# Sixteen of the 128 rows of wo's first load taken over by GpSimd, and sixteen small loads set among the large ones: a decode step with windowed attention

## The chip, the cores and the metric

The program runs on one core of one Trainium2 chip. A core has five engines with instruction streams of their own: TensorE (PE; its weight loads are PEld), VectorE (DVE), ScalarE (ACT), GpSimd (POOL) and SyncE (SP), and 16 DMA engines that move data between HBM and the on-chip memory SBUF, which has 128 partitions. The metric is the device time of one execution in microseconds, lower is better; a time is the median of several executions.

## What is computed

One token is decoded for two sequences (B = 2, D = 512). The token is normalised, goes through attention over the last 4096 positions of a cache and an output projection, and is gated by a small MLP:

```python
xn = _layernorm(x, axis=-1)
q = (x @ wq)                       # x here is xn; 32 heads of 128
k = k_cache[:, :, Sk - W:, :]      # Sk = 32768, W = 4096, 8 kv heads, repeated 4 times
v = v_cache[:, :, Sk - W:, :]
p = _softmax(einsum("bhqd,bhkd->bhqk", q, k) * Dh ** -0.5)
s = einsum("bhqk,bhkd->bhqd", p, v) -> (B, 1, 4096) @ wo
g = _silu(_B_ref(xn, w_in, w_sp, b_sp, w_out))
return x + s * g
```

All is float32. Read from HBM are the windows of k and v (32 MB each), wq and wo (8 MB each), w_in (3.5 MB) and w_out (1.75 MB).

## The kernel before, in words

**Loads.** Every large tensor passes through `ring`, a pool of four slots of 32 KB per partition (line 76, `slot` at line 81). In order: win, wout, two halves of wq, then the key and value windows, then wo. A *unit* is one sequence and two of its eight kv heads, so there are eight units (NU = 8). `load_unit` (line 114) loads the keys or the values of one unit, 128 rows of 32 KB, 4 MB in one transfer. The loop at line 416 issues k0, k1, v0, k2, v1, ... k7, v6, v7. Since four slots hold everything, each load from the fifth on waits until the slot's last content has been used: by VectorE's transposes for keys (`turn`, line 305), by TensorE for values (`values`, line 366).

After that comes wo (4096 x 512), split so that partition p holds the rows 32p to 32p + 31, in 32 blocks. It takes three slots, in pieces of 8 and 8 blocks, of 8, and of 4, 2, 1 and 1 (lines 424 to 434). A piece of 8 blocks is 128 partitions by 16 KB. After the second piece x is loaded once more in another layout (`x4`).

**Queues.** All these loads are issued by SyncE, in the order of the code. The names `pe`, `dve`, `act` and `sp` wrap an engine in `InOrder` (line 27), which pins each instruction behind the one before it on its engine; the profile therefore shows most instructions under line 37, the helper's call. `nc.gpsimd` is used without that wrap. ScalarE issues three tiny loads at the start. GpSimd builds masks at the start (lines 125 to 142: `make_identity`, then the memsets of xnT, ones, hT and others) and has nothing to do afterwards.

**Compute.** For each unit the keys are transposed by VectorE, multiplied by TensorE, and the softmax is made one unit behind (lines after 438). The last values give oT. Then 28 blocks of wo go into the bank `part` and the last four into `so` (lines 480 to 497), two small VectorE operations apply the gate and add x, and SyncE stores the result (line 501).

Of the kernel before, what the change touches and what calls it, by code (L numbers as in the profile page):

```python
# [9 lines left out]
F32 = mybir.dt.float32  # L10
# [4 lines left out]
P = 128  # L15
# [27 lines left out]
def kernel(  # L43
# [13 lines left out]
    nc = tc.nc  # L57
    pe, dve, act, sp = (InOrder(tc, e) for e in (nc.tensor, nc.vector, nc.scalar, nc.sync))
    B, _, D = x.shape
    _, HKV, SK, _ = k_cache.shape  # L60
# [8 lines left out]
    NU = B * HKV // 2  # L69
# [7 lines left out]
    cst = ctx.enter_context(tc.tile_pool(name="cst", bufs=1))  # L77
# [3 lines left out]
    def slot(name):  # L81
        return ring.tile([P, SLOT], F32, tag="slot", name=name)
# [18 lines left out]
    for a in range(2):  # L101
        t = slot(f"wq{a}")
# [7 lines left out]
    def by_group(t):  # L110

        return bass.AP(tensor=t.tensor, offset=t.offset, ap=[[DC, G], [D, B], [1, DC]])

    def load_unit(cache, u, name):

        b, w = divmod(u, NU // B)
        t = slot(f"{name}{u}")
        first = cache[b, 2 * w, SK - W :, :]
        src = bass.AP(tensor=first.tensor, offset=first.offset, ap=[[SLOT, P // 2], [SK * DH, 2], [1, SLOT]])
        sp.dma_start(t, src)  # L120
        return t.rearrange("p (j d) -> p j d", d=DH)
# [288 lines left out]
    for n in range(NU):  # L410
# [2 lines left out]
        u.b, u.w = divmod(n, NU // B)  # L413
        units.append(u)

    for n in range(NU + 1):
        if n < NU:
            units[n].k = load_unit(k_cache, n, "k")
        if n > 0:
            units[n - 1].v = load_unit(v_cache, n - 1, "v")  # L420

    wo_v = wo.rearrange("(p j) d -> p j d", j=32)
    blocks = []
    pieces = ((8, 8), (8,), (4, 2, 1, 1))
    j = 0
    for i, piece in enumerate(pieces):
        t = slot(f"wo{i}").rearrange("p (j d) -> p j d", d=D)
        at = 0
        for n in piece:
            sp.dma_start(t[:, at : at + n, :], wo_v[:, j : j + n, :])  # L430
            blocks += [(t, at + a) for a in range(n)]
            at, j = at + n, j + n
            if j == 16:
                sp.dma_start(x4[0:P:16, :], by_group(x))

    prev = old = None
    last = units[-1]
# [44 lines left out]
    for n in range(EARLY):  # L482
        t, a = blocks[n]
# [5 lines left out]
    for n in range(EARLY, 32):  # L489
        if n == LATE:  # L490
            spread_quarters(so, parts, start=False, stop=False)
        t, a = blocks[n]
# [37 lines left out]
```

## Time and profile before

| what | value |
|---|---|
| time, median of 3 runs | 217.89 us (217.43 to 218.01) |
| time of the profiled execution | 217.89 us |
| its span, first to last instruction | 216.1 us |
| PE, DVE, ACT, POOL busy | 153.6, 108.6, 44.0, 2.6 us |
| read from HBM | 89.40 MB, 414 GB/s over the span |
| loads of k: issue to landing | 26.0 us (8 loads of 4 MB) |
| loads of v: issue to landing | 30.6 us (8 loads of 4 MB) |
| SP's DMA instructions | 29 |

The span is what the trace covers; some 1.8 us of the measured time lie around it. In the profile, times in windows and timelines count from the start of the span. "SPq" is SyncE's instruction queue, where a load is issued; q1 is the queue of the DMA engines that these loads fill, q10 the one of ScalarE's loads, q8 and q14 carry the program's own code. "DMA share" is the mean busy share of the 16 DMA engines in a window; in short windows it can stand a little above 1. A line such as `k<-in_A_k_cache_dram` names the tile written and the tensor read.

### The profile page before, as it was taken

To read this page: it belongs to the slowest core of one execution; us is meant where nothing else is said; L and a number is where in the kernel's file an instruction comes from. 1 tells how busy PE (TensorE), PEld (TensorE's weight loads), DVE (VectorE), ACT (ScalarE), POOL (GpSimd) and SP (SyncE) were. 2 spreads that over 40 slices of the span, in tenths; PEclk is the share of its full clock that TensorE was granted. 3 is DMA by queue.
4 is the path that set the end of the run, shared out by engine and by line. 5 is a ranking of instruction groups with operands and counts; after the bars stand their busy time and mean duration, and the time that the engine had idled before them with its cause. 6 is when DMAs were issued, how large, how long until landed. Compare 5 with 4: busy or idle time off the path is not lost.

```text
span 216.1 us, 2228 instructions
## 1 busy us (share of the span) xinstructions
PE 153.6 (71%) x866; PEld 43.1 (20%) x866; DVE 108.6 (50%) x176; ACT 44.0 (20%) x109; POOL 2.6 (1%) x14
## 2 busy tenths in 40 slices
PE   0173185518959957994995699459959967997963
PEld 0121121101212212221221222222222212231311
DVE  2505402569788079338806941685479089331001
ACT  5003310002231331043131304120331241242001
POOL 4000000000000000000000000000000000000000
PEclk9998579955997995899799589856996996999698
DMA  6999999999999999999999999999999999999990
GB/s 256 425 437 467 406 438 422 431 443 419 455 400 473 397 455 412 431 437 419 450 403 461 412 461 403 443 419 425 449 412 452 412 455 412 443 397 425 424 368 26
DMA packets 3929, 89.54 MB, mean 414 GB/s; under 512 B 446, under 2 KB 462, under 8 KB 848
## 3 DMA queue, kind: packets, MB, share of 16 engines
q1 hardware_dynamic: 3912, 89.40, 96.7%
q8 instruction: 7, 0.11, 0.2%
q10 hardware_dynamic: 8, 0.00, 0.0%
q14 instruction: 2, 0.02, 0.0%
HBM read 89.40 MB, written 0.00 MB: 414 GB/s over the span
## 4 chain that ended last, share of the span: by engine, by line
DMA 52%; PE 28%; DVE 18%; issue 1%; DVEq 0%; SPq 0%
DMA k<-in_A_k_cache_dram 38%; DVE kt L37 15%; PE sh L37 9%; PE s L37 8%; DMA wo<-in_A_wo_dram 8%; PE acc L37 6%; DMA win<-in_B_w_in_dram 5%; PE z L37 2%; PE mo L37 1%; PE so L37 1%; DVE m L37 1%; DVE pT L37 1%; PE oT L37 0%; DVE mx L37 0%; PE col L37 0%
## 5 line engine op out<-in xcount | busy, mean ns | idle before, releaser
L37 DVE STREAM_TRANSPOSE kt<-k 128x2048 f32<-128x2048 f32 x32 | 72.7, 2295 | 41.7 <-DMA k<-in_A_k_cache_dram 35.7
L37 PE MATMUL sh<-kt,qbd 128*32 128x512 f32 x256 | 41.4, 710 | 18.4 <-DVE kt L37 18.4
L37 ACT ACTIVATE shs<-sh 128x512 f32<-128x512 f32 x32 | 19.1, 597 | 119.3 <-PE sh L37 119.3
L37 PE MATMUL s<-shs,add_dq 128*128 128x512 f32 x64 | 40.0, 732 | 0.0
L37 PE MATMUL acc<-v,pT 128*32 128x512 f32 x256 | 31.9, 640 | 0.2 <-DVE pT L37 0.2
L37 PEld LDWEIGHTS s<-shs,add_dq 128*128 128x128 f32 x64 | 11.0, 215 | 30.1 <-issue 25.7
L37 PEld LDWEIGHTS sh<-kt,qbd 128*32 128x32 f32 x256 | 6.5, 115 | 38.8 <-issue 24.5
L37 PEld LDWEIGHTS acc<-v,pT 128*32 128x32 f32 x256 | 7.7, 119 | 25.5 <-issue 18.3
L37 PE MATMUL mo<-l,same_r 128*128 128x2 f32 x16 | 3.7, 299 | 10.6 <-ACT p L37 10.6
L37 ACT ACTIVATE o<-acc,wd 128x128 f32<-128x128 f32 x32 | 9.1, 372 | 3.4 <-PE acc L37 3.4
L37 PE MATMUL part<-wo,oT 128*32 128x512 f32 x56 | 8.0, 708 | 2.0 <-DMA wo<-in_A_wo_dram 1.7
L37 ACT ACTIVATE p<-s,nb 128x256 f32<-128x256 f32 x16 | 7.6, 490 | 7.2 <-DVE nb L37 6.9
L37 PE MATMUL q_ps<-wq,xnT 128*32 128x512 f32 x64 | 7.3, 594 | 2.3 <-DMA wq<-in_A_wq_dram 2.3
L37 PE MATMUL col<-o,sel 128*32 128x512 f32 x16 | 8.3, 601 | 0.4 <-ACT o L37 0.4
L37 PE MATMUL z<-win,xnT 128*32 128x448 f32 x32 | 5.3, 836 | 4.5 <-DMA win<-in_B_w_in_dram 4.5
L37 DVE TENSOR_REDUCE m<-s 128x2 f32<-128x512 f32 x8 | 5.4, 670 | 4.9 <-PE s L37 4.9
L37 DVE TENSOR_TENSOR res<-so,gate 128x128 f32<-128x128 f32 x1 | 0.3, 291 | 11.7 <-PE so L37 11.7
L37 PE MATMUL y<-wout,hT 128*32 128x512 f32 x14 | 3.3, 993 | 3.8 <-issue 3.8
L37 DVE STREAM_TRANSPOSE pT<-p 128x512 f32<-128x512 f32 x8 | 5.4, 674 | 1.2 <-ACT p L37 1.2
L37 ACT ACT_TABLE_LOAD x4 | 5.1, 1283 | 1.9 <-issue 1.9
L37 PE MATMUL xnT_ps<-ident,xn 2*128 2x2 f32 x4 | 0.6, 252 | 6.9 <-DVE xn L37 6.9
L37 PEld LDWEIGHTS mo<-l,same_r 128*128 128x128 f32 x16 | 3.0, 233 | 12.2 <-ACT p L37 12.2
(106 smaller groups left out, 63.2 us busy)
## 6 DMA issues: line engine op xcount, KB each, us to landing
k<-in_A_k_cache_dram SPq DMA_DIRECT2D x8, 4096.0 KB, 26.0
v<-in_A_v_cache_dram SPq DMA_DIRECT2D x8, 4096.0 KB, 30.6
wq<-in_A_wq_dram SPq DMA_DIRECT2D x2, 4096.0 KB, 29.7
wo<-in_A_wo_dram SPq DMA_DIRECT2D x3, 2048.0 KB
win<-in_B_w_in_dram SPq DMA_DIRECT2D x1, 3584.0 KB
wout<-in_B_w_out_dram SPq DMA_DIRECT2D x1, 1792.0 KB, 15.0
wo<-in_A_wo_dram SPq DMA_DIRECT2D x1, 1024.0 KB
wo<-in_A_wo_dram SPq DMA_DIRECT2D x1, 512.0 KB, 18.0
```

The lines of the kernel that those rows point to most:

```text
L37: return self.tc.keep_in_program_order(call(*args, **kwargs))
```

## The change

Three things are added or altered.

- *Small loads from SyncE.* `load_rows(n)` loads n rows of 128 bytes of x (n from 1 to 16) into a tile `rows` that nothing reads. One follows most of the large loads of the loop over units (n = 2 to 14 and 1), and two follow wo's third piece (15 and 16). They stand in SyncE's pinned order.
- *The first piece of wo in two parts.* SyncE loads partitions 0 to 111 of it. The partitions 112 to 127 are loaded by GpSimd (`load_rest`) in six transfers of 4, 2, 3, 2, 2 and 3 rows of 16 KB.
- *Fillers.* Before, between and after these stand seven GpSimd transfers of 2, 1, 5, 3, 1, 5 and 15 rows of 4 bytes of x, into a tile `few` that nothing reads. GpSimd's transfers are not pinned in program order.

The bytes of wo, k and v are the same, and so is all arithmetic.

```diff
@@ -413,25 +413,61 @@
         u.b, u.w = divmod(n, NU // B)
         units.append(u)
 
+    rows = cst.tile([16, 16, 32], F32, tag="rows", name="rows")
+
+    def load_rows(n):
+        sp.dma_start(rows[:n, n - 1, :], bass.AP(tensor=x.tensor, offset=x.offset, ap=[[32, n], [1, 32]]))
+
     for n in range(NU + 1):
         if n < NU:
             units[n].k = load_unit(k_cache, n, "k")
+            if n > 0:
+                load_rows(2 * n)
         if n > 0:
             units[n - 1].v = load_unit(v_cache, n - 1, "v")
+            if n < NU - 1:
+                load_rows(2 * n + 1)
+            elif n == NU - 1:
+                load_rows(1)
+
 
     wo_v = wo.rearrange("(p j) d -> p j d", j=32)
     blocks = []
     pieces = ((8, 8), (8,), (4, 2, 1, 1))
+    HEAD = 112
+    few = cst.tile([16, 16], F32, tag="few", name="few")
+    steps = ((0, 2), (4, 0), (0, 1), (2, 0), (0, 5), (3, 0), (0, 3), (2, 0), (0, 1), (2, 0), (0, 5), (3, 0), (0, 15))
+    assert sum(n for n, _ in steps) == P - HEAD
+
+    def load_rest(dst, src):
+        p = HEAD
+        for i, (n, skip) in enumerate(steps):
+            if n > 0:
+                nc.gpsimd.dma_start(dst[p : p + n], src[p : p + n])
+                p += n
+            else:
+                nc.gpsimd.dma_start(
+                    few[:skip, i : i + 1], bass.AP(tensor=x.tensor, offset=x.offset, ap=[[32, skip], [1, 1]])
+                )
+
     j = 0
     for i, piece in enumerate(pieces):
         t = slot(f"wo{i}").rearrange("p (j d) -> p j d", d=D)
         at = 0
         for n in piece:
-            sp.dma_start(t[:, at : at + n, :], wo_v[:, j : j + n, :])
+            dst, src = t[:, at : at + n, :], wo_v[:, j : j + n, :]
+            if j == 0:
+                sp.dma_start(dst[:HEAD], src[:HEAD])
+                load_rest(dst, src)
+            else:
+                sp.dma_start(dst, src)
             blocks += [(t, at + a) for a in range(n)]
             at, j = at + n, j + n
             if j == 16:
                 sp.dma_start(x4[0:P:16, :], by_group(x))
+            if j == 24:
+                load_rows(15)
+                load_rows(16)
 
     prev = old = None
     last = units[-1]
```

## The prediction

> **What bounds the kernel now.** I read the page first: the 40 slices, the DMA queues and the chain that ended last.
>
> ```profile
> span 216.1 us, 2228 instructions
> ...
> DMA  6999999999999999999999999999999999999990
> ...
> q1 hardware_dynamic: 3912, 89.40, 96.7%
> q8 instruction: 7, 0.11, 0.2%
> ...
> DMA 52%; PE 28%; DVE 18%; issue 1%; DVEq 0%; SPq 0%
> ```
>
> The DMA engines are full from the second slice to the last but one. The queue that SyncE feeds (q1) moves 89.40 MB in 96.7% of 16 engines' span: 89.40 MB / (0.967 x 16 x 216.1 us) = 26.7 GB/s for one engine, so a row of 16 KB (one partition of half of wo's first slot) takes 16384 / 26.7 = 0.61 us of its engine. The chain of waits gives only 52% to DMA, but its waits alternate with work that runs under the stream, so the stages by window say more:
>
> ```profile
> core 0: us, PE busy (x) PEld busy (x) DVE busy (x) ACT busy (x) POOL busy (x), PEclk, DMA share, GB/s
> ...
> 2.00:212.00 210.00, 152.79 (x854) 42.82 (x858) 107.42 (x172) 43.87 (x109) 1.18 (x4) 0.85 0.99 425
> ```
>
> From 2 to 212 us the engines are busy 99%. No faster arithmetic shortens this; what sets the end is when the last of the 16 engines has moved its share. The chain's last pieces show the tail behind it:
>
> ```profile
> 193.00 18.05 DMA wo<-in_A_wo_dram
> 211.05 0.04 issue
> 211.09 1.25 PE so L37 x32
> 212.34 0.01 issue
> 212.35 0.47 PE so L37 x8
> ```
>
> The output projection follows the last loads of wo. How evenly the engines finish is seen in quarter-microsecond windows (column before the last: busy share of 16 engines):
>
> ```profile
> 209.50:209.75 0.25, 0.00 (x0) 0.00 (x0) 0.00 (x0) 0.00 (x0) 0.00 (x0) 1.00 1.07 410
> 209.75:210.00 0.25, 0.14 (x4) 0.15 (x8) 0.00 (x0) 0.00 (x0) 0.00 (x0) 1.00 0.74 279
> 210.00:210.25 0.25, 0.25 (x4) 0.01 (x2) 0.00 (x0) 0.00 (x0) 0.00 (x0) 1.00 0.52 197
> 210.25:210.50 0.25, 0.25 (x8) 0.00 (x0) 0.00 (x0) 0.00 (x0) 0.00 (x0) 1.00 0.55 213
> 210.50:210.75 0.25, 0.25 (x4) 0.00 (x0) 0.00 (x0) 0.00 (x0) 0.00 (x0) 1.00 0.47 180
> 210.75:211.00 0.25, 0.17 (x4) 0.00 (x0) 0.00 (x0) 0.00 (x0) 0.00 (x0) 1.00 0.41 156
> 211.00:211.25 0.25, 0.16 (x8) 0.16 (x12) 0.00 (x0) 0.20 (x1) 0.00 (x0) 1.00 0.38 147
> 211.25:211.50 0.25, 0.25 (x16) 0.21 (x8) 0.00 (x0) 0.25 (x1) 0.00 (x0) 1.00 0.28 107
> 211.50:211.75 0.25, 0.25 (x15) 0.05 (x8) 0.00 (x0) 0.14 (x1) 0.00 (x0) 1.00 0.07 25
> 211.75:212.00 0.25, 0.25 (x12) 0.25 (x16) 0.00 (x0) 0.00 (x0) 0.00 (x0) 1.00 0.02 8
> ```
>
> It is a staircase. Half of the engines (0.52) have nothing left at about 210.0, six (0.38 x 16) still work at 211.2, the last stops near 211.9: the early half waits almost 2 us for the late ones, though all got the same bytes. The seven packets on q8 load code: 0.2% of 16 x 216.1 us is 6.9 us, 1.0 us each, and whichever engine carries one falls behind by about that. That fits six or seven late engines.
>
> **The change part by part.** The profiled run took the median's own 217.89 us: 216.1 us of span and 1.79 us around it. The sum is made against that.
>
> (a) *A row fewer on the late engines.* SyncE loads 112 of 128 rows, seven an engine where it was eight; GpSimd brings the other 16 in six transfers of 4, 2, 3, 2, 2 and 3, with seven fillers of 2 to 15 tiny rows between, as if to steer each onto chosen engines. If the steering holds, the late engines keep one row less: -0.61 us, and the early ones, with one more, end at 210.0 + 0.61, still ahead. The staircase area from 209.75 on is 0.86 us of all 16 engines, so a perfect levelling would end at 210.6, 1.3 us sooner; one row cannot reach that. I take -0.61; from 0 (nothing shifted) to -0.61.
>
> (b) *Small loads.* Sixteen more SyncE loads of 1 to 16 rows of 128 bytes: 136 rows, 8.5 per engine on average, at most 16 on one. Their price comes from the output store, eight rows of 512 bytes and the counter writes of its four engines, 12 packets:
>
> ```profile
> 214.50:215.50 1.00, 0.00 (x0) 0.00 (x0) 0.00 (x0) 0.00 (x0) 0.00 (x0) 0.50 0.02 4
> ```
>
> 0.02 x 16 us / 12 is 0.027 us a packet. A row and its counter write are 0.05 us; 8.5 of them +0.45 us on the engine that ends last, from +0.05 (one) to +0.86 (sixteen). What the issues cost SyncE is in its timeline, the list of DMA issues and its waits:
>
> ```profile
> 170.15 0.66 SPq L37 DMA_DIRECT2D x<-in_A_x_dram  x1
> ...
> k<-in_A_k_cache_dram SPq DMA_DIRECT2D x8, 4096.0 KB, 26.0
> ...
> SPq L37 <- DMA k<-in_A_k_cache_dram: 26.2, 8, 5.3
> ```
>
> On SyncE each issue takes up to 0.66 us (the small load of x), and a big load behind it starts that much later. It is hidden by the queue: a 4 MB load needs 4194304 / 16 / 26.7 = 9.8 us of the engines and lands 26.0 us after its issue, so some 16 us of other loads lie ahead. Without that cover all sixteen issues would cost 10.6 us. SyncE already waits for earlier loads (26.2 us in 8 waits) before it overwrites one of four slots; should the small loads make a counter come round sooner, the load then waited for is about the one whose slot is refilled anyway, so I add nothing for it. Only the last 2048-byte pieces of wo could be held until the first pieces have landed, and those lie 4 MB ahead of them in the stream.
>
> (c) *Thirteen GpSimd transfers.* No transfer of that engine is in this trace. If each also leaves a counter write on every engine, 13 x 0.027 = +0.35 us; if only where it moves rows, about 0.1. I take +0.2. The timelines of SyncE, TensorE and GpSimd:
>
> ```profile
> 169.29 0.81 SPq L37 DMA_DIRECT2D wo<-in_A_wo_dram  x2
> ...
> 201.23 5.04 PE L37 MATMUL part<-wo,oT 128*32 128x512 f32 x32 [0.35 <-issue]
> ...
> 2.23 0.95 POOL L142 MEMSET oT<- 128x1024 f32 x1
> ...
> 0.87 0.20 POOL L127 MEMSET xnT<- 128x128 f32 x1
> 1.10 0.29 POOL masks.py:199 TENSOR_SCALAR_AFFINE_SELECT ident<-ident 128x128 f32<-128x128 f32 x1
> ```
>
> GpSimd is idle from 3.2 us on (2.23 + 0.95). Its real transfers wait for the same release of the slot as SyncE's, at 169.29; nothing stands behind them there, and TensorE first uses wo at 201.2, so their issue time costs nothing.
>
> (d) *Where the 16 rows land.* They go to 16 neighbouring partitions while the stream is at 99%. Until now each engine wrote rows that only it wrote at that time, all engines at full pace. Now several engines fill the same few partitions that others are filling. The trace has no such case. Bounds: nothing, if only the engine's own pace counts; and 16 x 0.61 = 9.8 us if the rows follow one another through one path and hold its regular engine back all the while. The nearest row is one transfer of this change: its largest has four neighbouring rows, and if these share one path with that path's own stream, it is put back by 4 x 0.61 = +2.45 us. I take this, as between no sharing and all on one the four are what the change itself issues together, and no cover exists: the stream has no gap in which an engine could catch up, and a late engine ends the kernel.
>
> [...]
>
> Sum: -0.61 + 0.45 + 0.2 + 2.45 = +2.5 us, **220.4 us**. Its own range: with the small terms at their bounds and (d) between 1.2 (half of the four rows meet traffic) and twice 2.45, 218.6 to 223.4.
>
> **The rivals.**
> 1. *It works: not slower.* The moved rows run freely; the late six end 0.61 us sooner. For it: every transfer in the trace runs at one pace, and the list fits the staircase: fillers and rows dealt in turn round 16 engines give seven engines two rows, two one and seven none. It decides as long as fewer than 0.61 / 0.027 = 22 small packets fall on the engine that ends; at the middle values 0.65 us they cancel it. 217.3 to 217.9; I say 217.6.
> 2. *The change doesn't do what it says.* The code makes the identity mask before it clears xnT, but the last two rows above show L127 ahead of masks.py:199: on that engine the order of the program is not kept. Fillers wait for nothing, real rows for a slot until 169 us; if the fillers all go first, nothing is steered, the late engines keep what they had, and without (d) (b) and (c) remain: +0.65, 218.5 (217.9 to 219.1).
> 3. *Each GpSimd transfer stalls the engines as a code load does.* A q8 packet takes 1.0 us against 0.61 for 16 KB: 0.38 more. Thirteen on every engine: 4.9 us, with (b) and without gain +5.4, 223.3. Against it: the small loads of ScalarE at the start leave no hole in the slices.
> 4. *The 112 rows collide as well.* Seven rows an engine no longer fall on the partitions that an engine had to itself. If each waits for one other row, 7 x 0.61 = 4.3 us more than the forecast: 224.7. [...]
>
> **How the numbers follow.** Forecast 0.38, rival 1 0.20, rival 2 0.15, rival 3 0.12, rival 4 0.15. A measurement of this kernel tells about 0.3% (0.65 us) from no change. Faster by more needs rival 1 with almost no small packets, or more levelling than a row: 0.09. Within 0.3%: the rest of rival 1 and most of rival 2, 0.25. Slower: 0.66. The range goes from 217.3 (rival 1's best) to 225.0 (rival 4); outside lie some 0.1 on either side. It is wide because two cases of no loss hold a third of the chance.
>
> **What would show it.** Right: a dip in DMA share or GB/s between 170 and 197 us, when the 16 rows and the 112 come, a staircase that begins later and is longer than 2 us, and last loads of wo at about 214.4. Rival 1: the same start of the staircase, steeper, over by 211.4. Rival 2: fillers on the timeline near 3 us, and the staircase as it was. Rival 3: low DMA share wherever a GpSimd transfer is issued, fillers too. Rival 4: wo's first pieces land 4 us late, with engines short of full share until then. The forecast is wrong if the share stays 0.99 from 170 to 200 us and the end moves by less than 1 us; (b) is wrong if shares drop around the small loads all along.

## The result and the profile after

The changed kernel takes 234.82 us (median of 4 executions, 234.29 to 236.5) beside 217.95 us for the kernel before (4 executions, 217.43 to 218.16). The ratio is 1.0791, 95% interval 1.0731 to 1.0851: 16.9 us slower. The profiled execution took 234.29 us.

The page of the changed kernel: its span, the 40 slices and the DMA queues (packets, MB, share of 16 engines' span).

```profile
span 232.4 us, 2267 instructions
...
DMA  7999999999999999999999999999999999999910
GB/s 252 419 457 445 434 407 426 440 445 440 400 440 437 445 412 423 440 446 427 401 440 440 443 417 418 440 446 434 403 420 330 367 355 285 228 279 383 363 74 8
...
q1 hardware_dynamic: 4168, 89.16, 94.2%
q0 software_dynamic: 416, 0.26, 0.5%
```

Up to slice 30 (about 174 us) nothing differs from before, though 14 of the sixteen small loads lie there. Then GB/s falls to 228 while the row above still shows 9: the engines are as busy as before and move half as much. Busy share alone would have shown no loss. The new queue q0 is GpSimd's: thirteen transfers left 416 packets, 32 each, whether they carried 1 row or 15.

The same in three stretches. Windows of the kernel before, then of the changed kernel (the last two columns are DMA share and GB/s):

```profile
168.00:188.00 20.00, 16.94 (x80) 4.29 (x72) 11.25 (x13) 5.64 (x14) 0.00 (x0) 0.91 1.02 437
188.00:208.00 20.00, 17.21 (x122) 5.27 (x124) 3.47 (x11) 3.33 (x12) 0.00 (x0) 0.91 0.97 412
208.00:216.00 8.00, 4.01 (x60) 1.20 (x52) 0.58 (x2) 0.60 (x1) 0.00 (x0) 0.90 0.34 130
```

```profile
168.00:188.00 20.00, 16.61 (x79) 4.30 (x72) 11.25 (x13) 5.64 (x14) 3.07 (x6) 0.91 1.02 371
188.00:208.00 20.00, 7.31 (x50) 2.12 (x52) 2.57 (x9) 2.19 (x8) 0.00 (x0) 0.72 0.98 270
208.00:216.00 8.00, 6.71 (x36) 2.15 (x28) 0.75 (x2) 1.14 (x4) 0.00 (x0) 0.84 0.98 391
216.00:224.00 8.00, 6.14 (x40) 1.75 (x44) 0.14 (x1) 0.00 (x0) 0.00 (x0) 0.79 0.64 254
224.00:232.00 8.00, 3.85 (x60) 1.20 (x52) 0.58 (x2) 0.60 (x1) 0.00 (x0) 0.94 0.05 18
```

At the stream's 425 GB/s the missing bytes are worth (437 - 371) x 20 / 425 = 3.1 us in the first stretch and (412 - 270) x 20 / 425 = 6.7 us in the second. The span grew by 16.3 us, so another 6.5 us are tail: from 216 to 224 us only 0.64 of the engines have anything left.

The timeline of the changed kernel, GpSimd and SyncE's issues:

```profile
3.14 3.74 POOL L449 DMA_DIRECT2D few<-in_A_x_dram  x7
...
169.18 0.80 SPq L37 DMA_DIRECT2D wo<-in_A_wo_dram  x2
169.44 3.07 POOL L446 DMA_DIRECT2D wo<-in_A_wo_dram  x6 [162.56 <-PE acc L37]
...
192.76 25.84 SPq L37 DMA_DIRECT2D wo<-in_A_wo_dram  x4
```

All seven fillers left at 3 us, 166 us ahead of the rows between which the code has them. The end of the chain of waits:

```profile
167.17 38.40 DMA v<-in_A_v_cache_dram
205.57 0.02 issue
205.59 21.26 DMA wo<-in_A_wo_dram
226.85 0.04 issue
226.89 1.24 PE so L37 x32
```

The last values take 38.40 us from issue to landing where a load of v took 30.6 before, and the load of wo that ends this chain lands at 226.85 instead of 211.05. SyncE waits too (us in total, times, longest):

```profile
SPq L37 <- DMA v<-in_A_v_cache_dram: 14.4, 2, 12.5
...
SPq L37 <- DMA wo<-in_A_wo_dram: 12.0, 2, 7.6
```

So its last three loads of wo are issued at 205.59, 213.51 and 218.27, where the last one went out at 193.95 before. This is not what costs the time: the engines were still 0.94 busy from 216 to 220 us, and the run below without small loads and fillers, in which only one load was issued that late (at 206.51), takes as long.

### The profile page after: what moved, and what is told of

It is laid out like the page before. It is cut to its first block, busy times and chain, and to the rows that moved or that the text cites. A ratio compares the mean times of both kernels' runs of the same rounds, so it can differ in the third digit from the quotient of the medians.

```text
span 232.4 us, 2267 instructions
## 1 busy us (share of the span) xinstructions
PE 159.0 (68%) x866; PEld 44.3 (19%) x866; DVE 108.5 (47%) x176; ACT 44.0 (19%) x109; POOL 9.4 (4%) x27
## 4 chain that ended last, share of the span: by engine, by line
DMA 57%; PE 24%; DVE 14%; issue 3%; ACT 1%; DVEq 0%
DMA k<-in_A_k_cache_dram 27%; DMA v<-in_A_v_cache_dram 17%; DVE kt L37 11%; DMA wo<-in_A_wo_dram 9%; PE sh L37 5%; DMA win<-in_B_w_in_dram 5%; PE s L37 4%; PE q_ps L37 4%; PE acc L37 4%; PE z L37 2%; PE y L37 2%; PE so L37 1%; PE mo L37 1%; DVE u L37 1%; DVE pT L37 1%
## 5 line engine op out<-in xcount | busy, mean ns | idle before, releaser
L37 PE MATMUL acc<-v,pT 128*32 128x512 f32 x256 | 34.5, 684 | 12.7 <-DMA v<-in_A_v_cache_dram 12.7
L37 PEld LDWEIGHTS acc<-v,pT 128*32 128x32 f32 x256 | 8.3, 125 | 40.3 <-issue 32.3
L37 DVE TENSOR_REDUCE heads<-col 32x128 f32<-32x512 f32 x2 | 1.3, 662 | 20.4 <-PE col L37 20.4
L446 POOL DMA_DIRECT2D wo<-in_A_wo_dram x6 | 3.1, 520 | 162.6 <-PE acc L37 162.6
L37 PE MATMUL q_ps<-wq,xnT 128*32 128x512 f32 x64 | 9.4, 751 | 0.0
```

The lines of the kernel that those rows point to most:

```text
L37: return self.tc.keep_in_program_order(call(*args, **kwargs))
L446: nc.gpsimd.dma_start(dst[p : p + n], src[p : p + n])
```

## The experiments

Fourteen kernels. Where one execution was made it says so; the kernel before beside them took 217.73 us (13 executions, 217.47 to 218.38) for the first eight, 217.97 (9) for the next four and 217.81 (3) for the last two.

**Each part of the change alone.** First the sixteen small loads without the rest: wo's first piece is one load again.

```diff
-                sp.dma_start(dst[:HEAD], src[:HEAD])
-                load_rest(dst, src)
+                sp.dma_start(dst, src)
```

> The sixteen small loads alone; the first piece of wo is one transfer of 128 rows again. Three theories stand. T1, shared ways: engines that write into the same few partitions share their way in, so the loss of 16.9 us comes from where the 112 rows and the 16 rows land. T2: each GpSimd transfer stalls the engines whatever it carries. T3: the small loads cost it. T1 and T2 expect +0.3 to +0.9 us here (8.5 rows per engine at 0.05 us), T3 most of 16.9 us.

217.81 us (10 executions), ratio 0.9999, interval 0.9988 to 1.001. The small loads cost nothing that can be measured.

Then the first piece in two parts, without GpSimd, small loads or fillers: 112 and 16 rows, or 64 and 64, both issued by SyncE.

```diff
-            sp.dma_start(t[:, at : at + n, :], wo_v[:, j : j + n, :])
+            dst, src = t[:, at : at + n, :], wo_v[:, j : j + n, :]
+            for rows in ((0, 112), (112, P)) if j == 0 else ((0, P),):    # or ((0, 64), (64, P))
+                sp.dma_start(dst[slice(*rows)], src[slice(*rows)])
```

> No small loads, no GpSimd: SyncE loads the first piece of wo as 112 rows and then 16 rows. T1 expects +5 to +10 us: seven rows an engine at up to twice 0.61 us (+4.3), and 16 rows that meet in four ways (+2.5) on engines that have fallen out of step. T2 and T3 expect +0.5 us or less.

> No small loads, no GpSimd: SyncE loads the first piece of wo as two halves of 64 rows, four rows an engine in each. T1 expects each half to reach only half of the ways into SBUF, so that the piece takes up to 9.8 us instead of 4.9: about +5 us, with 16 KB packets of about 1.2 us. If only an engine's own pace counts, 0 to +0.2 us and packets of 0.61 us.

224.86 us and 224.41 us (one execution each): +7.1 and +6.7 us for a second transfer of the same bytes. Windows of the two halves:

```profile
188.00:192.00 4.00, 4.00 (x33) 1.18 (x36) 1.40 (x5) 0.34 (x1) 0.00 (x0) 1.00 1.02 291
192.00:196.00 4.00, 2.90 (x30) 1.05 (x26) 1.18 (x4) 1.85 (x8) 0.00 (x0) 1.00 0.98 209
196.00:200.00 4.00, 3.60 (x24) 0.83 (x16) 0.00 (x0) 1.14 (x4) 0.00 (x0) 1.00 0.96 205
200.00:204.00 4.00, 1.44 (x9) 0.96 (x8) 0.89 (x2) 0.00 (x0) 0.00 (x0) 1.00 0.98 242
204.00:208.00 4.00, 3.06 (x16) 0.61 (x16) 0.00 (x0) 0.00 (x0) 0.00 (x0) 0.63 0.99 419
```

Busy 0.96 to 0.98, moving 205 to 242 GB/s: about half the pace for 12 us, from 192 to 204, where the kernel before moved 426 GB/s, and full pace (419) again right after. That a half of the rows reaches only half of the ways into SBUF, and that 16 rows meet in four, was T1's supposition: the windows show the pace, and no run shows a way or how many there are. The loss is larger than the +5 us expected, since more than the piece is slowed: it has 128 packets of 16 KB, and 163 took over 0.8 us.

Next the change without small loads and fillers, so that the split and GpSimd's six transfers remain (both calls of `load_rows` and the filler branch of `load_rest` do nothing).

> The change without its small loads and without the seven fillers: 112 rows from SyncE, 16 rows by six GpSimd transfers. T1 expects nearly all of the loss, +14 to +17 us. T2, by transfers (6 of 13), about half, +7 to +8 us. T3 expects under +2 us.

234.64 us (one execution), +16.9: the whole loss. So neither fillers nor small loads have a part in it. The split explains 7.1; what GpSimd adds was still open.

**What GpSimd's transfers cost beside a whole piece.** The kernel before, with eight more GpSimd transfers of four rows of 8 KB into a spare tile while the last values stream in; once four neighbouring partitions each, once four apart by four.

```diff
...
+    def extra_rows(u):
+        gp.tensor_copy(tick, u.wd[:, 0:1])
+        for rows in [slice(p, p + 4) for p in (80, 84, 88, 92, 112, 116, 120, 124)]:   # or slice(p, p + 13, 4), p = 0, 16, ..
+            gp.dma_start(spare[rows], wo_v[rows, 0:4, :])
...
+            if prev.n == 5:
+                extra_rows(prev)
```

> The kernel before, its first piece of wo whole, plus eight GpSimd transfers of four neighbouring rows of 8 KB (partitions 80 to 95 and 112 to 127, 256 KB in all) at the point where the change's rows came, into a tile that nothing reads. The change without small loads and fillers lost 16.9 us, the split piece alone 7.1; 9.8 us are left for GpSimd's rows. T1 (ways shared by where a row lands) expects +5 to +10 us here, packets of the stream beside the rows slowed. T4 (the rows are cheap; only on top of the split piece do they cost) expects +0.6 to +1.5 us, the extra bytes.

> The same with the four rows of each transfer four partitions apart, over all 128 partitions: same engine, queue, count and bytes, only the places differ. T1 expects much less than with neighbours, +0.6 to +2 us. T2' (16 KB of rows on GpSimd's queue stall the engines wherever they land) expects the same loss as with neighbours.

222.88 and 221.48 us (one execution each), +5.2 and +3.8. The 256 KB more are worth 0.6 us of the stream. The 1.4 us between the two are no more than what two executions of one slowed kernel can differ by (230.18 and 231.5 further down), so it is not shown that neighbouring partitions cost more here. Spread rows do not leave the stream alone either: 105 of its 32 KB packets took over 1.35 us, with neighbours 81, where 1.22 is usual. 3.8 us are there in either case, so neighbouring partitions cannot be all of it.

**Steering and number of transfers.** The change with GpSimd's transfers pinned in the order of the code, fillers between the rows:

```diff
+    gp = InOrder(tc, nc.gpsimd)
...
-                nc.gpsimd.dma_start(dst[p : p + n], src[p : p + n])
+                gp.dma_start(dst[p : p + n], src[p : p + n])
```

> The change with GpSimd's thirteen transfers in the order of the code, so that the fillers stand between the rows and steer them as they read. T1 expects 232 to 237 us: which engine carries a row does not matter beside where it lands. If the loss came from a wrong dealing of rows to engines, it falls to 224 us or less.

234.07 us (one execution), +16.3. Fillers in their places change nothing in the time. Next, without small loads and fillers, the 16 rows in one GpSimd transfer instead of six:

```diff
-    steps = ((0, 2), (4, 0), (0, 1), (2, 0), (0, 5), (3, 0), (0, 3), (2, 0), (0, 1), (2, 0), (0, 5), (3, 0), (0, 15))
+    steps = ((16, 0),)
```

> No small loads, no fillers, and the 16 rows in one GpSimd transfer instead of six. T1: the same 16 rows land in the same places, so at least the 7.1 us of the split piece and some of the other 9.8, 226 to 234 us. T2 (a price per transfer) expects a sixth of the 9.8 us on top of the 7.1: 226.5 us.

225.68 us (one execution), +8.0. Six transfers cost 9.0 us more than one with the same rows. That could be a price of each transfer, or of its being short; the next two tell them apart. First six GpSimd transfers again, each over all 16 rows and one or two of the blocks; then the portions of 4, 2, 3, 2, 2 and 3 rows, but all by SyncE.

```diff
-                nc.gpsimd.dma_start(dst[p : p + n], src[p : p + n])
+                for c, m in ((0, 2), (2, 1), (3, 1), (4, 2), (6, 1), (7, 1)):
+                    nc.gpsimd.dma_start(dst[p : p + n, c : c + m], src[p : p + n, c : c + m])
```

```diff
+            cuts = (0, 112, 116, 118, 121, 123, 125, P) if j == 0 else (0, P)
+            for a, z in zip(cuts, cuts[1:]):
+                sp.dma_start(dst[a:z], src[a:z])
```

> The 16 rows come by GpSimd in six transfers, each over all 16 rows and one or two of the eight blocks, so every transfer has 16 packets and gives every DMA engine the same; 112 rows by SyncE, no fillers, no small loads. Theory E (a GpSimd transfer is filled up to 16 packets, 32 with the counters, and begins at the same engine each time, so that transfers of 2 to 4 rows pile up on the first engines): no pile, as with one transfer, 225.7 us (224.5 to 227.5). Theory T (each GpSimd transfer costs 1.6 to 1.8 us whatever it carries): five transfers more, 225.7 + 5 x 1.75 = 234.4.

> 112 rows and then the 16 rows in the same six portions (4, 2, 3, 2, 2, 3), all by SyncE; no GpSimd, no fillers, no small loads. If short transfers pile rows on the first engines, for this queue too: engines 0 and 1 get six rows, 2 gets three, 3 one, where one transfer gives one to each; five rows more of 0.6 to 1.2 us at the late engine over the 224.9 of 112 + 16 rows: 228 to 231. If GpSimd's queue is what costs: 224.9 (224 to 226).

225.2 us (2 executions, ratio 1.0331, interval 1.0301 to 1.0361): six GpSimd transfers cost no more than one, if each has 16 rows. 230.84 us (2 executions, 230.18 and 231.5, ratio 1.0589, interval 1.0518 to 1.0661): short portions cost 5.7 us more than 112 + 16 rows (12.9 against 7.1), without GpSimd. So shortness costs on either queue. The queue has a part as well: the same portions come to +16.9 by GpSimd and +12.9 by SyncE, where one transfer of 16 rows differs by 0.8. Why was not settled. Windows of the run with the six blocks, then of SyncE's short portions:

```profile
212.00:216.00 4.00, 2.14 (x16) 0.42 (x16) 0.00 (x0) 0.00 (x0) 0.00 (x0) 0.85 0.99 405
216.00:220.00 4.00, 3.64 (x52) 1.42 (x48) 0.01 (x1) 0.60 (x1) 0.00 (x0) 0.72 0.34 130
220.00:224.00 4.00, 0.00 (x0) 0.00 (x0) 0.57 (x2) 0.00 (x0) 0.00 (x0) 0.71 0.00 1
```

```profile
212.00:216.00 4.00, 3.06 (x24) 0.42 (x16) 0.00 (x0) 0.00 (x0) 0.00 (x0) 0.87 0.97 403
216.00:220.00 4.00, 1.08 (x12) 0.45 (x16) 0.00 (x0) 0.00 (x0) 0.00 (x0) 0.98 0.53 209
220.00:224.00 4.00, 3.83 (x32) 0.88 (x24) 0.00 (x0) 0.49 (x1) 0.00 (x0) 0.59 0.09 31
```

With 16 rows in each the engines stop together by about 217.4 (0.34 of 4 us past 216); with short portions 0.09 of the engines, one or two of the 16, still work between 220 and 224.

The changed kernel's own packets show which. The records don't name the engine, but nearly every packet starts within some nanoseconds of the end of another, so from 150 us on they fall into 16 chains, one for each engine. GpSimd's sixteen 16 KB packets (start in us) stand in four of them:

```
engine A: 173.2 177.7 181.3 185.0 187.3 191.0
engine B: 173.5 178.2 182.5 186.3 187.1 189.9
engine C: 173.6 181.0 188.9
engine D: 174.8
```

Six, six, three and one: what transfers of 4, 2, 3, 2, 2 and 3 rows give if each begins again at the same engine. In the pinned run, with fillers between the rows, two chains again hold eleven of the sixteen, so the fillers steered nothing. In the run with one transfer of 16 rows they lie in 15 of the 16 chains, one of them with two (a chain that was followed wrongly would look like that). The eight transfers of four 8 KB rows beside a whole piece then put eight rows on each of four engines (with neighbouring rows the chains show eight in each of four); at the 0.31 us that such a packet took there this is 2.5 of the 3.8 us.

Engine A can be read whole. From 171.96 to 212.54 us its packets follow one another without a gap: two loads with eight packets of 32 KB each, the seven rows of wo's first piece that SyncE leaves it, and GpSimd's six. The six took 4.8 us. The sixteen packets of 32 KB took 8.4 us more than at 1.218 us each, and the seven rows 3.7 us more than at 0.615. One row fewer saves 0.6. So this engine is 16.2 us behind by then, and the span grew by 16.3: about a quarter is the rows that piled up, the rest is packets of the stream that were held up.

**Placement.** SyncE again, the first piece in two transfers of 64 rows as above, but the even rows and the odd rows:

```diff
-            for rows in ((0, 64), (64, P)) if j == 0 else ((0, P),):
+            for rows in (slice(0, P, 2), slice(1, P, 2)) if j == 0 else (slice(0, P),):
```

> [...] Theory P (it costs that the engines meet on the same ways into the partitions): 217.5 to 219. Theory S (a split of the piece costs whatever rows go into which transfer): 224.4.

218.14 us (8 executions, ratio 1.0009, interval 0.9996 to 1.0021). Two transfers of the same size that between them alternate over all partitions cost nothing, against +6.7 us for the two halves: the loss comes with which rows stand together, not with the second transfer. In all these runs row p of wo goes to partition p, so none parts the place in SBUF from the place in HBM; that it is the ways into the partitions fits the pace of the halves, but is argued. The rows of its windows:

```profile
192.00:196.00 4.00, 3.82 (x41) 1.13 (x34) 1.18 (x4) 2.14 (x8) 0.00 (x0) 1.00 1.03 434
196.00:200.00 4.00, 3.33 (x20) 0.59 (x12) 0.21 (x1) 1.14 (x4) 0.00 (x0) 1.00 0.98 418
200.00:204.00 4.00, 3.12 (x20) 1.66 (x24) 0.68 (x2) 0.00 (x0) 0.00 (x0) 0.80 1.04 439
```

The median duration of a 16 KB packet on SyncE's queue says the same, in ns (the windows are in us):

```
before, 190 to 205 us             615
even and odd rows, 190 to 205     615
two halves, 192 to 203           1221
112 + 16 rows, 192 to 203        1160
changed kernel, 194 to 207       1136
```

Last, the change with spread rows: GpSimd loads rows 7, 15, .. 127, in one transfer or in six of 4, 2, 3, 2, 2 and 3 rows; or SyncE loads these too.

```diff
+                for rows in (slice(0, P, 2), slice(1, P, 4), slice(3, P, 8)):    # SyncE alone: slice(7, P, 8) as well
+                    sp.dma_start(dst[rows], src[rows])
+                nc.gpsimd.dma_start(dst[7:P:8], src[7:P:8])                      # or in six
```

> [...] Theory P with E: 217.5 to 219.5, the change done without a loss. Theory T or S: not under the 225.7 of one GpSimd transfer with 16 neighbouring rows.

> [...] If the 3.8 us that were left with GpSimd bringing rows 7, 15, .. belong to GpSimd's transfer: 217.5 to 219. If they belong to the split into four with 16 and 32 rows: 221.7.

> As the run with rows 7, 15, .. by one GpSimd transfer (221.7 us), but those 16 rows in six GpSimd transfers of 4, 2, 3, 2, 2 and 3 rows, as in the change. The pile alone, each of the five rows more on the late engine at its own 0.6 to 1.2 us: 224.8 to 227.7. If the pile is that dear only together with neighbouring partitions, or is made dearer by the split of the rest (9 us between one and six transfers there): 230.7. If it counts only with neighbouring partitions: 221.7.

One GpSimd transfer: 221.73 us (2 executions, ratio 1.0171, interval 1.01 to 1.0243), +3.8. SyncE alone: 220.4 us (2 executions, ratio 1.0121, interval 1.0092 to 1.0151), +2.6; so at most some 1.2 us belong to GpSimd, less than these intervals can tell, and the expectation that every spread split is free fell. With SyncE alone, too, packets were held up: 81 of the 384 packets of 16 KB took over 0.8 us, all between 192 and 199 us, which comes to 2.5 us for each engine on average. With even and odd rows it was one packet. In six: 225.87 us (2 executions, ratio 1.0373, interval 1.0325 to 1.0421), +8.1, which is 4.3 more than in one, 0.86 us for each of the five rows more on the late engines. No version beat the kernel before.

## Why the prediction was wrong

Forecast 220.4 us (217.3 to 225.0), measured 234.82: the direction right, the size far off. Taken in this order, the runs account for the 16.9 us so: 7.1 for the split into 112 and 16 rows, 0.8 for GpSimd in place of SyncE with one transfer (225.68 against 224.86, one execution each, so hardly told from nothing), 9.0 for six short transfers in place of one, nothing for small loads and fillers. The upper end of the sum's own range, 223.4, keeps (a) at -0.61; with (a) at its bound of 0 it is 224.0, which changes nothing here.

(a) *A row fewer on the late engines, -0.61: wrong in sign, and one of the two steps that failed.* It took the rows as dealt out over the engines. They were not: two engines got six more rows of 16 KB each. With 112 rows SyncE leaves seven an engine (so many stand in engine A's chain), so those two move 13 rows where they moved 8. The pile costs 4.3 us with spread rows, 5.7 as SyncE's portions, 9.0 in the change. On engine A the six rows took 4.8 us by themselves, and 12.0 us went into packets of the stream that were held up; a pile is dear where it also holds up the stream. How much of that is due to neighbouring partitions is only argued: no run has the change's pile beside a whole piece, and the same neighbouring rows cost 5.7 by SyncE and 9.0 by GpSimd.

Why GpSimd's short transfers begin at the same engine each time, no run shows. That SyncE's short portions pile up in the same way is inferred from their time, 230.84 against 224.86 us, and from their tail.

(b) *Small loads, +0.45: too much.* Measured 217.81 against 217.73 us. With 0.9988 as the lower end and 1.001 as the upper, they cost between -0.3 and +0.2 us. The price of a packet was too high: in the changed kernel's trace a row of 128 bytes took 13 ns and a counter write 9, so 0.02 us for both and not 0.05. That the last pieces of wo could be held until the first had landed came true (the waits above), and cost nothing.

(c) *Completions, +0.2: small, as said.* Thirteen GpSimd transfers instead of six make no difference that these runs can tell (234.82 against 234.64), nor six instead of one if all are full (225.2 against 225.68).

(d) *Where the 16 rows land, +2.45: the kind of loss right, the size a third, the other step that failed.* It looked only at the four rows of one GpSimd transfer. That four rows share one path, and that an engine had its partitions to itself before, as (d) and rival 4 suppose, no run shows: a packet's record names neither engine nor partition. The 112 rows are slowed too, as rival 4 had it, and the split alone costs 7.1 us. That this part was given 0.15 and not the main place is the error of judgement; even and odd rows against halves show it to be placement and not the second transfer. Rival 4's 224.7 lies near the 224.86 of the split alone partly by luck: 4.3 and 2.45 for rows that collide are 6.7 of the 7.1, but its other terms were not borne out, and it was meant for the whole change, which takes 234.82.

*Rivals.* 1 (it works) fell with (a). 2: its observation was right (fillers at 3.14 us), its consequence empty, since pinned fillers steer nothing either (234.07). 3 (each GpSimd transfer stalls the engines) fell: fillers cost nothing, and six full transfers cost no more than one. 4 was half of the answer; it should have been in the sum, though not for every split: even and odd rows in two transfers kept 418 to 439 GB/s.

*Signs.* Of "a dip in DMA share or GB/s between 170 and 197 us" only GB/s dipped, and on to 208. The staircase is longer than 2 us, as said, but for a reason that the forecast did not have.

## What to carry to other kernels

Load a tile over all its partitions at once: the whole piece was never beaten here (217.73 to 217.97 us). If it must be split, spread each part over all partitions, and measure it: even and odd rows cost nothing, four spread parts 2.6 us. A part of neighbouring partitions beside a full stream can halve the pace of everything while the engines look busy (two halves: 205 to 242 GB/s at 0.96 to 0.98 busy), so read GB/s beside the busy share. Count rows per DMA engine for each transfer by itself: here GpSimd's transfers of 2 to 4 rows left six, six, three and one of 16 rows on four engines, and the span grew by 16.3 us where the fullest that was read whole was 16.2 behind. Pin work that is to follow other work on an engine (unpinned, the fillers left 166 us ahead of the rows), and before steering anything by fillers, look in the packets whether the engine that gets the next row moves at all.

## What was not expected of the hardware

A busy DMA engine can be one that is held up: 0.96 to 0.98 busy at 205 to 270 GB/s (two halves, changed kernel), with the 16 KB packet at 1.1 to 1.2 us instead of 0.615. GpSimd's transfer always left 32 packets on its queue (416 for thirteen, 192 for six, 32 for one), whatever its rows. One transfer of 16 neighbouring rows by GpSimd held up the whole stream for a moment; the window of that run at its time:

```profile
168.00:172.00 4.00, 4.00 (x22) 1.06 (x14) 0.00 (x0) 1.80 (x5) 0.61 (x1) 1.00 1.09 434
172.00:176.00 4.00, 1.56 (x4) 0.14 (x2) 0.55 (x1) 0.43 (x2) 0.00 (x0) 1.00 1.15 188
176.00:180.00 4.00, 2.09 (x9) 0.46 (x10) 2.70 (x4) 0.04 (x1) 0.00 (x0) 0.69 0.79 336
```

From 434 to 188 GB/s for 256 KB: about (434 - 188) x 4 / 425 = 2.3 us of the stream for rows that are worth 0.6. The time is only 0.8 us over that of SyncE's 112 + 16 rows all the same, likely because the 16 rows are then out of the way of the 112: from 188 to 208 us this run has 332 GB/s, that one 286. Why packets were held up with SyncE's split into even rows, rows 1, 5, .., 3, 11, .. and 7, 15, .. (+2.6 us), where even and odd rows cost nothing, was not settled.
